# Transformer block on one core: first-group gate/up with plain products, second group nested as before, and another POOL cost in the planner

## The chip, the cores and the metric

The kernel runs on one core of a Trainium2 chip. The core has a matrix engine (TensorE, PE), a vector engine (VectorE, DVE), an activation engine (ScalarE, ACT), a general engine (GpSimd, POOL) and SyncE (SP), which issues most DMA transfers. Each engine has its own queue, and they wait for one another through semaphores. Matmul results land in PSUM, eight banks of 128 x 512 float32; all else on the core is in SBUF. The metric is the device time in microseconds (us) of one execution.

## What is computed

The reference is a block with modulation by a condition `c`, a linear attention and a gated feed-forward part, for 2048 rows of width 1024 and a hidden width of 3584:

```python
mod = (_silu(c) @ w_mod).reshape(c.shape[0], 6, 1, -1)   # sa, ca, ga, sb, cb, gb
h = _layernorm(x) * (1 + ca) + sa
x = x + ga * _A_ref(h, A_wqkv, A_wo)                     # linear attention, 32 heads
h = _layernorm(x) * (1 + cb) + sb
x = x + gb * _B_ref(h, B_w_gate, B_w_up, B_w_down)       # gelu(h @ w_gate) * (h @ w_up) @ w_down
```

The change lies in `h @ w_gate` and `h @ w_up`.

## The kernel before

**Order of the work.** All operations are first recorded in a plan (`Plan`). The matmuls of PE keep the order in which they were recorded. The orders of DVE, ACT, POOL and SP are worked out by the plan: `Plan.cost` gives each operation a cost, `sweep` runs a list schedule forward and backward over all operations, and the best order found is issued. So a cost that is changed for one engine can change the order on the other three, anywhere in the program. Helpers carry the line numbers: every DVE addition recorded through `tt_op` shows as L534, every copy of PSUM to SBUF through `fcopy` as L781.

**Stages.** First come queries, keys and values with the attention (`kvq_phase`, `merge_phase`), then the output projection with the second layer norm of the first group (`wo_phase`). Then, for each of two groups of 1024 rows, `gate_up(g)` and `down_out(g)`. The first group's gate/up has the late norm of the second group beside it (`late_norm`, one tile of 128 rows in a unit: ACT L1135, POOL L1136, ACT L1137, POOL L1138 to L1140, ACT L1141), and the preparation of weights for the down projection (`wd_sums`, in every other unit: ten DVE sums, whose results POOL stores to the scratch tensors `us` and `ts`; the SBUF slot for `us` is a single one).

**Products by Strassen and Winograd.** A product of two matrices, each in 2 x 2 blocks, is made with seven block products instead of eight, and sums of blocks before and after. `gate_up` runs over 14 units, gate and up in turn. A unit covers 256 hidden columns in two blocks, and each block product is eight matmuls: two halves e of 128 hidden columns (the weights are the stationary operand), four blocks of the contraction, and 512 rows moving (`mm_k`, L1284). The seven products of a unit are called P1 to P7 here; P1 is made at the end of the unit before it, beside P6 and P7. X, Z and Y are pairs of PSUM banks. P1 starts in Z, is copied from PSUM to PSUM by `seed` (ACT, L1338), and later products are added on both copies: P2 on one, P3, P4 and P6 one after another on the other, each read by ACT or DVE between (`direct`, `fcopy`, `comb`).

**Nested products.** A block product can itself be made with seven smaller ones (`Inner`, L1295): seven times two matmuls of 256 columns in the place of eight with 512. `INNER` says which products of a group are nested: before the change the first product, `b11`, in both groups (from unit 1 on) and the fifth, `t1`, in the second. A nested first product needs four more sums of weights per unit on DVE (`w_unit`), four sums of rows once per group (`rows_inner`), one PSUM copy (L1301) and two copies to SBUF on ACT, and two additions in PSUM on DVE (in `s32` and `s4`). Its steps are put between P6, P7 and the next unit's P2, and so are the two seeds: the last step `s6` and the second seed stand between P2(0) and P3(0) of the next unit.

Where the first product is plain, the branch that runs is:

```python
for e in range(2):
    mm_k(Z[e], w_next["a11"], e, h["b11"], True)
    P6(e)
    seed(X[e], Z[e])
P7(0)
P7(1)
```

**Memory.** SBUF is one tile, `mem`, that is cut by hand at offsets in KB. The sums of a nested product's rows lie at `yi_at`, those of its weights at `wi_rings` (from 7 and from 177). The `b11` quarter of the down projection's weights is loaded at 7 (`W_AT`), over the first of these rings.

Of the kernel before, what the change touches and what calls it, by code (L numbers as in the profile page):

```python
# [12 lines left out]
F16 = mybir.dt.float16  # L13
# [10 lines left out]
class Plan:  # L24
# [98 lines left out]
    def cost(self, op, outs, ins):  # L123

        size = lambda a: math.prod(d[1] for d in a.ap[1:])
        n = max(size(a) for a in (outs if op.eng == "PE" else outs + ins))
        psum = any(a.tensor.name.startswith("psum") for a in outs + ins)
        wide = any(a.dtype == FP32 and size(a) > 8 for a in outs + ins)
        ptrs = sum(size(a) == 1 for a in ins)
        if op.eng == "PE":  # L130
            op.cost = n / 2.4 + 2.5
            op.lat = op.cost + 165
            if op.fn == "matmul" and outs[0].ap[0][1] <= 32:
                op.cost /= 3.5
        elif op.fn.startswith("dma"):
            a = outs[0]
            op.cost, op.bytes = 1000 if op.eng == "POOL" else 450, math.prod(d[1] for d in a.ap) * (4 if a.dtype == FP32 else 2)
            op.bytes *= 2 if "accum_op" in op.kw else 1
            op.load = a.tensor.name.startswith("mem")
            if op.fn == "dma_start_transpose":  # L140
                op.cost, op.bytes = self.transpose
            op.lat = op.cost
        elif op.eng == "ACT":
            op.cost = (55 if psum else 112) + n / 1.2 + 85 * ptrs
            op.lat = op.cost + 115
            f = op.kw.get("func")
            op.table = "g" if f == AF.Gelu_apprx_tanh else "e" if f in (AF.Exp, AF.Ln) else None
        elif op.eng == "POOL":
            op.cost = op.lat = 700 + n / 0.5
        else:  # L150
            rate = 1.0
            if op.fn in ("tensor_scalar", "tensor_scalar_mul", "tensor_scalar_add", "tensor_copy") and not wide:
                rate = 1.0 if psum else 4.0
            elif op.fn == "tensor_tensor" and not wide:
                rate = 2.0
            op.cost = 69 + n / (0.96 * rate) + 61 * ptrs
            op.lat = op.cost + 83
# [119 lines left out]
def kernel(  # L277
# [39 lines left out]
    KH = KD // 2  # L317
# [57 lines left out]
    def at(off, shape, dt):  # L375
        return Ring(off, shape, dt, 1)()
# [43 lines left out]
    HB = TG // 2  # L420
# [42 lines left out]
    def quarters(n, shape, dt):  # L463
# [6 lines left out]
    f32_ring = Ring(158, [TG], FP32, 6)  # L470
    u_ring = Ring(170, [HB], FP32, 4)
    wi_rings = [Ring(7, [3, KH // 2, P], F16, 2), Ring(177, [3, KH // 2, P], F16, 2)]
    yi_at = [{"b11": at(174, [4, KH // 2, HB], F16)},
             {"b11": at(144, [4, KH // 2, HB], F16), "t1": at(148, [3, KH // 2, HB], F16)}]
    INNER = (("b11",), ("b11", "t1"))
    inner_done, h_inner = set(), {}
    p1v, p5v = at(158, [TT, NW], FP32), at(166, [TT, NW], FP32)
    c0_ring = Ring(174, [TG], F16, 3)
# [761 lines left out]
    def w_unit(g, n):  # L1240
# [12 lines left out]
        w = dict(a11=a11, a12=a12, a22=a22, s1=s1, s2=s2, s3=s3, s4=s4, inner={})  # L1253
        for name in INNER[g]:
            if n == 0 and name == "b11":
# [11 lines left out]
    def rows_inner(g):  # L1267
# [3 lines left out]
        inner_done.add(g)  # L1271
        for name in INNER[g]:
            y = h2[name]
# [445 lines left out]
```

## Time and profile before

| | |
|---|---|
| Median of 8 runs | 760.74 us (759.52 to 762.29) |
| Profiled execution, its own time | 760.0 us |
| Its span, first to last instruction | 758.2 us |
| PE busy | 735.7 us (97%), 4164 matmuls |
| DVE busy | 622.1 us (82%) |
| ACT busy | 412.4 us (54%) |
| POOL busy | 105.5 us (14%) |
| 128x512 matmul of L1284 | 1248, mean 379 ns |
| 128x256 matmul of L1295 | 560, mean 272 ns |
| Granted clock of TensorE | 1.00 |

[...]matmuls follow each other faster than they last, so the pace has to be read from their starts. The windows of a profile give the busy time of each engine in a stretch, in the order PE, weight loads (PEld), DVE, ACT, POOL, with the number of instructions, then clock, DMA share and GB/s. A line of the waits reads: who waited, for whom, total us, times, longest. In a timeline a bracket gives the idle time before an instruction and what ended it.

### The profile page before, as it was taken

How to read it: one execution, taken by the hardware profiler on the slowest of the kernel's cores; microseconds unless marked ns; L12 is line 12 of the kernel's file. 1: busy time of each engine (PE TensorE's matmuls, PEld its weight loads, DVE VectorE, ACT ScalarE, POOL GpSimd, SP SyncE). 2: the span in 40 equal slices, each digit the busy share in tenths (PEclk: the TensorE clock that was granted, in tenths of full speed). 3: DMA queues.
4: the chain of work that ended last, by engine and by line, in shares of the span. 5: the costliest groups of instructions: out<-in, count | busy, mean ns of one | idle time of the engine just before them, and what ended most of it. 6: DMA issues, size and time to landing. Idle time of an engine off the chain costs nothing.

```text
span 758.2 us, 11401 instructions
## 1 busy us (share of the span) xinstructions
PE 735.7 (97%) x4164; PEld 391.5 (52%) x4164; DVE 622.1 (82%) x1288; ACT 412.4 (54%) x697; POOL 105.5 (14%) x199
## 2 busy tenths in 40 slices
PE   5999999999999999989999999999999999999997
PEld 2454544453444445444445486645555555548664
DVE  7898986589897899899887779578889899897763
ACT  3675576668766578767565235016666666621000
POOL 1321433007121123141000001010000000000000
PEclk9999999999999999999999999999999999999999
DMA  9847167779389677876431999752323313399822
GB/s 314 299 116 248 38 154 165 291 293 173 98 235 324 210 261 277 295 256 216 131 107 49 288 288 301 257 185 87 112 64 104 112 57 112 101 271 293 272 110 75
DMA packets 140759, 144.78 MB, mean 191 GB/s; under 512 B 33440, under 2 KB 120864, under 8 KB 139936
## 3 DMA queue, kind: packets, MB, share of 16 engines
q1 hardware_dynamic: 124016, 106.31, 46.4%
q0 software_dynamic: 14336, 35.66, 14.8%
q10 hardware_dynamic: 2352, 2.10, 0.8%
q8 instruction: 32, 0.52, 0.3%
q14 instruction: 23, 0.19, 0.1%
HBM read 111.81 MB, written 32.24 MB: 190 GB/s over the span
## 4 chain that ended last, share of the span: by engine, by line
PE 76%; DVE 7%; ACT 5%; DMA 5%; issue 5%; POOL 1%; SPq 1%; POOLq 0%; DVEq 0%; ACTq 0%
PE psum L1284 25%; PE psum L1487 13%; PE psum L1531 8%; PE psum L836 6%; PE psum L1295 6%; PE psum L1176 6%; DVE mem L534 6%; PE psum L906 4%; PE psum L935 4%; DMA us<-mem 2%; DMA mem<-in_A_wqkv_dram 2%; DMA mem<-in_w_mod_dram 1%; PE psum L950 1%; PE psum L962 1%; DVE mem L975 1%
## 5 line engine op out<-in xcount | busy, mean ns | idle before, releaser
L534 DVE TENSOR_TENSOR mem<-mem 128x512 f16<-128x512 f16 (+11 forms) x633 | 291.9, 505 | 15.5 <-DMA us<-mem 5.4
L1284 PE MATMUL psum<-mem 128*128 128x512 f16 x1248 | 299.3, 379 | 2.8 <-ACT mem L781 1.0
L534 DVE TENSOR_TENSOR mem<-psum,mem 128x512 f16<-128x512 f32 (+4 forms) x260 | 192.1, 747 | 70.6 <-ACT mem L781 25.6
L781 ACT ACTIVATE mem<-psum 128x256 f32<-128x256 f32 (+2 forms) x228 | 123.3, 555 | 119.7 <-PE psum L1531 43.6
L1284 PEld LDWEIGHTS <-mem 128*128 128x128 f16 (+1 forms) x1248 | 122.0, 98 | 114.5 <-issue 5.2
L1487 PE MATMUL psum<-mem 128*128 128x512 f16 (+2 forms) x462 | 99.2, 373 | 0.5 <-DVE mem L534 0.5
L1295 PE MATMUL psum<-mem 128*128 128x256 f16 x560 | 89.5, 272 | 2.4 <-DVE psum L534 2.2
L1295 PEld LDWEIGHTS <-mem 128*128 128x128 f16 (+1 forms) x560 | 54.7, 98 | 48.1 <-issue 6.5
L1487 PEld LDWEIGHTS <-mem 128*128 128x128 f16 x462 | 45.2, 98 | 49.9 <-issue 0.7
L1338 ACT ACTIVATE psum<-psum 128x512 f32<-128x512 f32 x56 | 32.9, 587 | 62.1 <-PE psum L1284 31.5
L1531 PE MATMUL psum<-mem 128*128 128x256 f16 (+1 forms) x588 | 66.2, 273 | 0.0
L836 PE MATMUL psum<-mem 128*128 128x512 f16 (+1 forms) x280 | 62.5, 379 | 0.0
L1531 PEld LDWEIGHTS <-mem 128*128 128x128 f16 x588 | 57.6, 98 | 9.2
L1176 PE MATMUL psum<-mem 128*128 128x512 f16 x256 | 57.4, 379 | 0.6 <-DVE mem L534 0.6
L906 PE MATMUL psum<-mem 128*128 128x512 f16 x224 | 51.1, 379 | 0.1
L534 DVE TENSOR_TENSOR psum<-psum,mem 128x256 f32<-128x256 f32 x80 | 34.1, 426 | 11.6 <-ACT mem L781 11.5
L836 PEld LDWEIGHTS <-mem 128*128 128x128 f16 x280 | 27.0, 98 | 31.2
L1355 ACT ACTIVATE mem<-psum 128x512 f16<-128x512 f32 x56 | 33.3, 597 | 17.4 <-PE psum L1284 17.0
L1176 PEld LDWEIGHTS <-mem 128*128 128x128 bf16 x256 | 25.0, 98 | 31.0 <-issue 0.9
L906 PEld LDWEIGHTS <-mem 128*128 128x128 f16 (+1 forms) x224 | 21.5, 98 | 26.8 <-issue 2.1
L1365 ACT ACTIVATE mem<-mem 128x512 f16<-128x512 f16 x56 | 34.9, 629 | 0.5 <-DVE mem L534 0.3
L612 DVE BATCH_NORM_STATS2 mem<-mem 128x6 f32<-128x512 bf16 x48 | 30.9, 676 | 2.1 <-DMA mem<-in_A_x_dram 2.0
(127 smaller groups left out, 565.2 us busy)
## 6 DMA issues: line engine op xcount, KB each, us to landing
mem<-in_B_w_gate_dram SPq DMA_DIRECT2D x14, 1024.0 KB, 5.4
mem<-in_B_w_up_dram SPq DMA_DIRECT2D x14, 1024.0 KB, 5.9
mem<-in_w_mod_dram SPq DMA_DIRECT2D x24, 512.0 KB, 6.9
mem<-us SPq DMA_DIRECT2D x24, 448.0 KB, 8.0
mem<-in_A_x_dram SPq DMA_DIRECT2D x32, 256.0 KB, 3.7
ts<-in_B_w_down_dram POOLq DMA_DIRECT2D x28, 256.0 KB, 6.4
us<-mem POOLq DMA_DIRECT2D x7, 768.0 KB, 7.5
mem<-in_B_w_down_dram SPq DMA_DIRECT2D x12, 448.0 KB, 7.1
```

The lines of the kernel that those rows point to most:

```text
L534: ve.tensor_tensor(out=out, in0=a, in1=b, op=op)
L781: ac.activation(out=t, in_=ps, func=AF.Copy)
L836: te.matmul(ps, lhsT=A[:, k, i * P:(i + 1) * P], rhs=B[:, k, :], start=(start and k == 0), stop=(k == KH - 1), skip_group_check=True)
L906: te.matmul(o, lhsT=W[:, k, (j0 + i) * P:(j0 + i + 1) * P], rhs=h_form(a, k), start=(start and k == 0), stop=(k == KH - 1), skip_group_che ...
L1176: te.matmul(psw[:, half, :], lhsT=pqT[b][:, g, tl * P:(tl + 1) * P], rhs=Wp[:, g, half * NW:(half + 1) * NW], start=(g == 0), stop=(g == K ...
L1284: te.matmul(ps, lhsT=a[:, k, e, :], rhs=b[:, k, :], start=(start and k == 0), stop=(k == KH - 1), skip_group_check=True)
L1295: te.matmul(ps, lhsT=self.x[a][:, k, :], rhs=self.y[y][:, k, :], start=(start and k == 0), stop=(k == KH // 2 - 1), skip_group_check=True)
L1338: ac.activation(out=z, in_=x, func=AF.Copy)
L1355: ac.activation(out=o, in_=ps, func=AF.Gelu_apprx_tanh)
L1365: ac.activation(out=o, in_=o, func=AF.Gelu_apprx_tanh)
L1487: te.matmul(psm[:, q, c], lhsT=A[:, i, q * P:(q + 1) * P], rhs=wt[:, i, c], start=(start and i == 0), stop=(i == NPR - 1), skip_group_chec ...
L1531: te.matmul(ps[:, q, :], lhsT=a[:, k, q * P:(q + 1) * P], rhs=y[:, k, :], start=(start and q == 0 and k == 0), stop=(k == NPR // 2 - 1), s ...
```

## The change

The first group's gate/up makes all of its seven products with `mm_k`; the second group keeps the first and fifth nested. In the planner, a POOL operation of up to eight elements a partition is taken at 500 instead of about 702 ns, and larger ones at 250 + n / 0.46 instead of 700 + n / 0.5. Lines after 472 move up by one.

```diff
         elif op.eng == "POOL":
-            op.cost = op.lat = 700 + n / 0.5
+            op.cost = op.lat = 500 if n <= 8 else 250 + n / 0.46
...
     wi_rings = [Ring(7, [3, KH // 2, P], F16, 2), Ring(177, [3, KH // 2, P], F16, 2)]
-    yi_at = [{"b11": at(174, [4, KH // 2, HB], F16)},
-             {"b11": at(144, [4, KH // 2, HB], F16), "t1": at(148, [3, KH // 2, HB], F16)}]
-    INNER = (("b11",), ("b11", "t1"))
+    yi_at = [{}, {"b11": at(144, [4, KH // 2, HB], F16), "t1": at(148, [3, KH // 2, HB], F16)}]
+    INNER = ((), ("b11", "t1"))
```

In instructions: PE has 104 matmuls of 512 columns more and 182 of 256 fewer, DVE 82 instructions fewer, ACT 39 fewer; POOL and SP have as many as before.

## The prediction

> **What bounds the kernel now.** I first read the busy table and the chain of waits on the page: the chain that ended last is 76% TensorE (PE), and its largest line is L1284, the plain gate/up matmul. Then I took the busy time by stage. The stages were found by the first and last start of the lines that only one of them has. The last row is the second group, the first is the first group's gate/up, and the middle one is its down projection.
>
> ```profile
> core 0: us, PE busy (x) PEld busy (x) DVE busy (x) ACT busy (x) POOL busy (x), PEclk, DMA share, GB/s
> ...
> 253.50:427.50 174.00, 169.11 (x864) 84.33 (x863) 148.46 (x326) 117.63 (x220) 30.49 (x63) 1.00 0.62 206
> 427.50:508.00 80.50, 80.50 (x520) 50.66 (x518) 63.75 (x115) 19.62 (x30) 6.02 (x9) 1.00 0.86 254
> 508.00:673.40 165.40, 165.09 (x947) 92.44 (x946) 146.18 (x337) 106.13 (x221) 1.43 (x2) 1.00 0.36 108
> ```
>
> The reader should see that PE is at full clock and nearly always busy, but that the first group needs 174.0 us where the second, with more nesting, needs 165.4. To know how much of that is PE's own work I need the pace of one matmul, which the chain in order of time gives where PE runs freely:
>
> ```profile
> 340.54 1.73 PE psum L1284 x8
> ...
> 460.97 1.53 PE psum L1531 x14
> ```
>
> Eight matmuls with 512 columns take 1.73 us, 216 ns each; fourteen with 256 columns take 1.53 us, 109 ns each. In the first group unit 0 is plain, 56 x 216 = 12.1 us, and 13 units have six plain products and one nested: 48 x 216 + 14 x 109 = 11.9 us. That sums to 166.8 us, so 174.0 - 166.8 = 7.2 us are stalls. In the second group the same sum is 164.0 us, so only 1.4 us are stalls there, although two products are nested and DVE is 88% busy (146.2 of 165.4; first group 148.5 of 174.0, 85%).
>
> Where the 7.2 us are, I read from the starts of successive PE matmuls in the first group. Fifteen start more than 60 ns late, together 7.2 us. Laid against the kernel's PE order they are: six times the product P2(1) behind the seed copy on ACT, 0.26 to 0.42 us each, 1.9 us in all; six times the nested steps s7 and s6 behind the PSUM additions of s32 and s4 on DVE, 3.0 us in all; twice P7 behind DVE work of the unit, 1.2 us; once P6(0) behind a copy on ACT, 1.2 us. The table of waits shows the parts of these that stand out as idle PE, and what held DVE:
>
> ```profile
> PE psum L1295 <- DVE psum L534: 2.0, 4, 0.7
> PE psum L1284 <- ACT mem L781: 1.0, 1, 1.0
> PE psum L1284 <- DVE mem L534: 0.8, 2, 0.6
> PE psum L1284 <- ACT psum L1338: 0.7, 3, 0.3
> ...
> DVE mem L534 <- DMA us<-mem: 5.4, 3, 3.0
> ```
>
> One example of each, from the timeline:
>
> ```profile
> 269.47 0.61 ACT L1338 ACTIVATE psum<-psum 128x512 f32<-128x512 f32 x1
> 270.13 1.24 PE L1284 MATMUL psum<-mem 128*128 128x512 f16 x5 [0.25 <-ACT psum L1338]
> ...
> 327.75 0.42 DVE L534 TENSOR_TENSOR psum<-psum,mem 128x256 f32<-128x256 f32 x1
> 328.22 0.38 PE L1295 MATMUL psum<-mem 128*128 128x256 f16 x2 [0.51 <-DVE psum L534]
> ...
> 335.64 1.64 POOL L1136 TENSOR_SCALAR mem<-mem 128x1 f32<-128x1 f32 x1
> 337.31 1.15 ACT L1137 ACTIVATE mem<-mem 128x1024 f16<-128x1024 bf16 x1 [1.33 <-POOL mem L1136]
> 339.08 1.02 PE L1284 MATMUL psum<-mem 128*128 128x512 f16 x4 [1.00 <-ACT mem L781]
> ```
>
> The first two pairs are handovers that only the nested product has; the last triple is the late norm, POOL holding ACT and ACT holding a copy that PE needs.
>
> **What the Trainium skill says.** "TensorE: Matmul & The Clock Gate", section "Back-to-back issue gap", gives N/2.4 + 2.5 ns between matmuls, 109 ns for 256 columns and 216 ns for 512, and adds that a real stream at 512 runs at about 131 ns. The trace agrees with the formula and not with the 131. "Perfetto Trace Analysis", "Identifying the Most-Contended Engine", warns that matmul busy time is a bad measure; agreed here, as 169.1 us busy stand over 166.8 us of work and hide part of 7.2 us of stalls. "PSUM — Partial Sum Buffer", "Engine vs sequencer instructions", says that ScalarE, VectorE and GpSimdE queues are strictly first in, first out. The trace agrees: DVE stood 3.0 us at one addition for a `us` store and all behind it waited.
>
> **The change, part by part.**
>
> PE work. Removed: 13 units x 14 matmuls of 256 columns = 182 x 109 ns = 19.9 us. Added: 13 x 8 of 512 columns = 104 x 216 ns = 22.5 us. Net +2.6 us, all on the path, since PE sets the pace of this stage. The second group's PE order stays as it is.
>
> DVE. Removed per unit: four sums of weights, 128x256, 0.28 us each by the rows of that shape, and two PSUM additions of 0.43 us: 1.98 us, 25.7 us over 13 units; and the four sums of `rows_inner(0)`, 4 x 0.42 = 1.7 us. The stage's DVE time falls from 148.5 to about 123 us.
>
> ACT. Removed per unit two copies of 0.38 us and one PSUM copy of 0.37 us: 14.7 us in all. The two seed copies per unit, 0.59 us each, stay. Neither is PE time; their worth is in the stalls.
>
> Stalls that go. In the nested form the seed copy stands between s6 and P2(1) with one group of four matmuls (0.86 us) to cover it, and s32's and s4's addition, which follows a copy on ACT, has 1.73 us before s7 or s6. In the plain form seed(X[e]) follows P6(e), and five groups, 4.3 us, lie before the next unit's P2(e) needs it. ACT's or DVE's `direct` (0.60 or 0.69 us) comes first, then the seed (0.59 us): covered with 3 us to spare. If that cover goes, a late seed again costs its 0.3 to 0.4 us. So 1.9 + 3.0 = 4.9 us go. What is late next is the copy of P3 or P4, with 1.73 us before P4 or the following product overwrites its bank and 0.60 us to do; it is the plain part's tightest handover in both kernels.
>
> Stalls that stay. P7's 1.2 us and P6's 1.2 us come from DVE held by the single `us` buffer and from POOL and ACT in the late norm. Neither is removed. Bounds: 0 if the freed 2 us of DVE per unit let DVE catch up, 4.6 if they double. I take 2.3, unchanged.
>
> `rows_inner(0)`. Its four sums stand in DVE's queue during the output projection, right before the stretch in which the chain runs over DVE from 234.87 to 239.2 and PE then starts 0.81 us late at 239.27 behind a PSUM eviction. Taking 1.7 us out ahead of it should clear that: -0.8 us (bounds 0 and -0.8).
>
> POOL's cost in the planner, 702 to 500 ns for the one-column operations. It changes no instruction, only the orders of DVE, ACT, POOL and SP, and PE's not at all. The measured ones average 0.38 us (from 0.20 to 0.64 by row), so the planner still errs on the late side and ACT shouldn't stand at POOL more often. Orders before the first group move by a place or two; the number of matmuls between each release and its reader there is nearly the same in both. I take 0, bounds -1 and +2, two ACT operations of 1.06 us placed ahead of a needed copy.
>
> Loads. All of them remain, with the same sizes. `b11` of the down projection no longer waits for the nested weights' slot; before it was issued at 415.89, took about 7.2 us and was wanted at 427.5, so it is hidden in both.
>
> Sum: +2.6 - 4.9 - 0.8 = -3.1 us. The profiled execution, 758.2 us of span and 1.8 around it, 760.0 in all, becomes 756.9. The median shown, 760.74, lies 0.74 above, so I forecast 757.6 us.
>
> **The rivals.** About 0.2%, 1.5 us, is what a measurement of this kernel can tell from no change.
>
> A, forecast: nested-only stalls go, others stay: 757.6 us. Chance 0.55.
>
> B, the stalls go almost whole and the earlier stages gain: +2.6 - 7.2 - 0.8 = -5.4, 755.3 us. For it: DVE falls to about 72% of the stage. Against: the `us` wait and POOL's 1.64 us are not load. Chance 0.1.
>
> C, no change: part of what goes comes back at P3's and P4's copies, so that only about 2.6 of 8.0 us are gained: 760.7 us. For it: second group, with tighter handovers and the same DVE share, stalls only 1.4 us, so nesting alone is not the cause; a hold of 3.0 us on DVE is longer than any handover. Chance 0.2.
>
> D, slower: the cause of all first-group stalls is the hold by `us` stores and late norm, and the plain form merely takes it at another wait. The 7.2 us stay, nothing is gained at 239, and PE pays its 2.6 us: 763.3 us. It decides from where less than 1.1 us of stalls goes; the reordering's +2 would help it. Against: the six seed stalls recur in quiet units, at 270 and 408 too, with DVE not held. Chance 0.15.
>
> That the nested products stay in the first group is excluded by the order of instructions: PE has 78 matmuls fewer.
>
> **How the numbers follow.** A and B lie mainly in faster; A's own spread of about 1.7 us leaves a little to no change, D a little too. Faster 0.63, within 0.2% 0.21, slower 0.16. A's own range is 755.5 to 759.8. The wide one reaches from B, 755.4, into C and most of D: 755.4 to 762.8.
>
> **What would show it.** Right: the first group's gate/up lasts about 171.7 us with 169.3 us of matmul work (784 x 216 ns); waits on the seed and of L1295 on DVE are gone in it; DVE's busy time there is near 123 us; the late start at 239 is gone; the second group stays at 165.4. Wrong: stalls of over 5 us in the first group, at the writes after P3's and P4's copies or with DVE idle for `us`; or a stage before it that is over 1 us longer, which would put the reordering in the place of my zero.

## The result, and the profile after

The changed kernel takes 762.19 us (median of 18 runs, 759.52 to 763.99), the kernel before, run beside it, 759.6 us. The ratio is 1.0032, with a 95% interval of 1.0024 to 1.0040: slower by about 2.6 us, where I had forecast faster. The profiled execution took 763.52 us, 1.3 above the median, its span 761.7, against 760.0 and 758.2 before: 3.5 us more.

First the windows by stage, the view that the prediction shows for the kernel before, for the changed kernel: output projection, first group's gate/up, its down projection, second group's gate/up.

```profile
190.90:251.60 60.70, 60.23 (x280) 27.27 (x279) 50.26 (x80) 39.35 (x56) 11.97 (x22) 1.00 0.81 247
251.60:427.00 175.40, 171.65 (x785) 76.98 (x784) 129.60 (x248) 107.85 (x181) 34.90 (x63) 0.99 0.63 207
427.00:509.20 82.20, 80.58 (x519) 50.67 (x518) 67.67 (x126) 19.38 (x30) 6.03 (x9) 1.00 0.79 233
509.20:676.80 167.60, 165.77 (x948) 92.50 (x947) 140.26 (x326) 106.58 (x221) 1.42 (x2) 1.00 0.34 105
```

The first group's gate/up, where all removed instructions but the four sums of `rows_inner(0)` lay, is 1.6 us longer (175.45 by the starts of the first matmuls, 173.85 before). The two stages after it, which hold the same instructions as before, are longer too, by 1.8 us (82.22 for 80.44) and 2.1 us (167.57 for 165.46). PE reaches the gate/up 2.0 us earlier, at 251.55 for 253.51. The sum is -2.0 + 1.6 + 1.8 + 2.1 = +3.5 us. So 3.9 of the 5.5 us lost lie in stages from which the diff removes nothing, and the gain lies ahead of the gate/up, from where it removes only those four sums of DVE.

**The first group.** Matmul work is 169.3 us, as forecast, and the nested form's own stalls are gone. But 6.1 us of stalls stand in it, where I had left 2.3. Three lines of the waits of this stage:

```profile
ACT mem L1140 <- POOL mem L1139: 4.8, 4, 3.0
...
PE psum L1283 <- ACT mem L780: 3.6, 4, 2.2
ACT mem L1136 <- POOL mem L1135: 3.3, 4, 1.4
```

Before, ACT had one wait for POOL there:

```profile
ACT mem L1137 <- POOL mem L1136: 1.3, 1, 1.3
```

The place of the longest of PE's waits, in the timeline of the changed kernel:

```profile
344.35 1.06 ACT L780 ACTIVATE mem<-psum 128x512 f32<-128x512 f32 x2
344.52 0.75 POOL L1137 TENSOR_SCALAR mem<-mem 128x1 f32<-128x1 f32 x1 [1.35 <-ACT mem L1136]
...
345.99 0.60 POOL L1037 DMA_DIRECT2D us<-mem  x1 [0.72 <-DVE mem L533]
346.62 1.44 POOL L1138 TENSOR_TENSOR mem<-mem 128x1 f32<-128x1 f32 x1
348.14 0.26 POOL L1139 TENSOR_TENSOR mem<-mem 128x1 f32<-128x1 f32 x1
348.43 1.24 ACT L1140 ACTIVATE mem<-mem 128x1024 f16<-128x1024 bf16 x1 [3.02 <-POOL mem L1139]
349.58 1.06 ACT L780 ACTIVATE mem<-psum 128x512 f32<-128x512 f32 x2
...
350.21 8.11 PE L1283 MATMUL psum<-mem 128*128 128x512 f16 x29 [2.16 <-ACT mem L780]
```

Read it from the bottom. P6(0) waits for a copy of PSUM (L780) on ACT. The copy stands in ACT's queue right behind the late norm's L1140, which waits 3.02 us for POOL; and POOL had a store of `us` between two operations of the norm, which waited for DVE. From start to start the matmul is 2.3 us late. Three shorter waits for P3's copies add 1.7 us, and one more at P6 0.5 us. After the long one PE runs at half pace for a while, which costs another 1.7 us (the last section).

**The down projection.** PE has one stall in it. Here is ACT's part of the timeline, first before, then changed; L1156 and L1155 are the same line, the modulation of the second group's rows, which reads what the DMA transpose of the scratch tensor `xhs` brings.

```profile
447.29 0.60 ACT L781 ACTIVATE mem<-psum 128x512 f32<-128x512 f32 x1 [2.46 <-PE psum L1531]
448.81 0.60 ACT L781 ACTIVATE mem<-psum 128x512 f32<-128x512 f32 x1 [0.93 <-PE psum L1531]
449.31 3.62 ACT L1156 ACTIVATE mem<-mem 128x512 f16<-128x512 f16 x5
455.38 0.60 ACT L781 ACTIVATE mem<-psum 128x512 f32<-128x512 f32 x1 [2.45 <-DVE mem L534]
```

```profile
453.51 3.63 ACT L1155 ACTIVATE mem<-mem 128x512 f16<-128x512 f16 x5 [4.46 <-DMA mem<-xhs]
...
457.05 0.57 ACT L780 ACTIVATE mem<-psum 128x512 f32<-128x512 f32 x1
...
457.68 1.69 PE L1530 MATMUL psum<-mem 128*128 128x256 f16 x14 [1.61 <-ACT mem L780]
```

Five modulations wait 4.46 us for the transpose. The copy behind them starts 30.05 us after the stage's first matmul, where before it started after 28.02, and PE waits for this copy.

**The second group.** DVE waits for loads of weights five times, which it never did there before, and PE then waits for DVE or for ACT behind it. From the waits of the second gate/up, for all engines and for PE:

```profile
DVE mem L533 <- DMA mem<-in_B_w_gate_dram: 5.0, 5, 2.2
```

```profile
PE psum L1294 <- ACT psum L1300: 1.0, 3, 0.4
PE psum L1294 <- DVE psum L533: 0.7, 3, 0.3
```

Before, the table of PE's waits in this stage had one line, L1295 behind DVE, 0.2 us.

### The profile page after: what moved, and what is told of

Same layout as the page of the kernel before. It is cut to its first block, busy times and chain, and to the rows that moved or that the text cites. A ratio compares the mean times of both kernels' runs of the same rounds, so it can differ in the third digit from the quotient of the medians.

```text
span 761.7 us, 11075 instructions
## 1 busy us (share of the span) xinstructions
PE 739.1 (97%) x4086; PEld 384.0 (50%) x4086; DVE 600.5 (79%) x1206; ACT 402.6 (53%) x658; POOL 108.0 (14%) x199
## 4 chain that ended last, share of the span: by engine, by line
PE 74%; DVE 9%; DMA 7%; ACT 6%; issue 2%; POOL 1%; SPq 0%; DVEq 0%; POOLq 0%; ACTq 0%
PE psum L1283 25%; PE psum L1486 13%; DVE mem L533 7%; PE psum L1530 6%; PE psum L1175 6%; PE psum L905 5%; PE psum L835 5%; PE psum L1294 4%; PE psum L934 4%; DMA mem<-in_B_w_gate_dram 3%; PE psum L660 2%; DMA mem<-xhs 2%; DMA us<-mem 1%; PE psum L949 1%; DMA mem<-in_B_w_up_dram 1%
## 5 line engine op out<-in xcount | busy, mean ns | idle before, releaser
L1283 PE MATMUL psum<-mem 128*128 128x512 f16 x1352 | 312.4, 380 | 3.7 <-ACT mem L780 3.6
L533 DVE TENSOR_TENSOR mem<-mem 128x512 f16<-128x512 f16 (+12 forms) x577 | 279.6, 526 | 20.8 <-DMA mem<-in_B_w_gate_dram 7.4
L1283 PEld LDWEIGHTS <-mem 128*128 128x128 f16 (+1 forms) x1352 | 132.6, 98 | 142.2 <-issue 7.5
L780 ACT ACTIVATE mem<-psum 128x512 f32<-128x512 f32 (+2 forms) x202 | 112.9, 576 | 113.9 <-PE psum L1530 43.0
L1337 ACT ACTIVATE psum<-psum 128x512 f32<-128x512 f32 x56 | 32.7, 583 | 64.4 <-PE psum L1283 31.2
L1294 PE MATMUL psum<-mem 128*128 128x256 f16 x378 | 59.0, 272 | 1.8 <-ACT psum L1300 1.0
L1175 PE MATMUL psum<-mem 128*128 128x512 f16 x256 | 57.4, 379 | 0.5 <-DVE mem L533 0.5
L1294 PEld LDWEIGHTS <-mem 128*128 128x128 f16 (+1 forms) x378 | 36.9, 98 | 31.3 <-issue 5.3
L905 PE MATMUL psum<-mem 128*128 128x512 f16 x224 | 51.1, 379 | 0.3 <-ACT mem L850 0.2
L905 PEld LDWEIGHTS <-mem 128*128 128x128 f16 (+1 forms) x224 | 21.5, 98 | 27.2 <-issue 2.6
L533 DVE TENSOR_TENSOR psum<-psum,mem 128x256 f32<-128x256 f32 x54 | 23.0, 427 | 10.3 <-ACT mem L780 10.2
```

The lines of the kernel that those rows point to most:

```text
L533: ve.tensor_tensor(out=out, in0=a, in1=b, op=op)
L780: ac.activation(out=t, in_=ps, func=AF.Copy)
L905: te.matmul(o, lhsT=W[:, k, (j0 + i) * P:(j0 + i + 1) * P], rhs=h_form(a, k), start=(start and k == 0), stop=(k == KH - 1), skip_group_che ...
L1175: te.matmul(psw[:, half, :], lhsT=pqT[b][:, g, tl * P:(tl + 1) * P], rhs=Wp[:, g, half * NW:(half + 1) * NW], start=(g == 0), stop=(g == K ...
L1283: te.matmul(ps, lhsT=a[:, k, e, :], rhs=b[:, k, :], start=(start and k == 0), stop=(k == KH - 1), skip_group_check=True)
L1294: te.matmul(ps, lhsT=self.x[a][:, k, :], rhs=self.y[y][:, k, :], start=(start and k == 0), stop=(k == KH // 2 - 1), skip_group_check=True)
```

## The experiments

Theory 1: the loss is one of order. The plan works out anew what DVE, ACT, POOL and SP do after one another, over the whole program, whenever operations or a cost change; in the new order operations that wait for slow things (POOL, a transpose, a weight load) stand ahead of ones that PE needs. Rivals: the plain products as such bring new stalls, or the loads that now run earlier collide.

The stages of all runs, in us, from the starts of the first gate/up or down matmul in one profiled execution each; "start" is PE's arrival at the first gate/up. The second down projection took 81.3 in every one. With an unchanged order a stage still differs between executions: start by 2.2, the first gate/up by 1.4 (by 2.1 in the changed kernel's order), the down projection by 0.9 (by 1.3 in the old order, through e9), the second gate/up by 0.5. The medians are of 14 to 22 executions, in e6, e11 and e12 of five.

| kernel | start | gate/up 1 | down 1 | gate/up 2 | median | ratio to before, 95% |
|---|---|---|---|---|---|---|
| before | 253.51 | 173.85 | 80.44 | 165.46 | | |
| changed | 251.55 | 175.45 | 82.22 | 167.57 | 762.19 | 1.0032 (1.0024 to 1.0040) |
| e1 plain products only | 253.68 | 172.12 | 81.74 | 167.95 | 760.55 | 1.0010 (0.9998 to 1.0021) |
| e2 POOL cost only | 253.51 | 172.47 | 81.69 | 165.38 | 760.84 | 1.0032 (1.0014 to 1.0049) |
| e3 changed, old order after group 1 | 253.10 | 176.65 | 80.44 | 165.49 | 760.79 | 1.0015 (1.0004 to 1.0026) |
| e4 changed, copies ahead | 253.71 | 172.17 | 81.31 | 167.24 | 760.61 | 1.0023 (1.0014 to 1.0031) |
| e5 both | 253.34 | 172.64 | 80.44 | 165.46 | 758.39 | 0.9979 (0.9972 to 0.9987) |
| e6 before, new order after group 1 | 254.84 | 173.17 | 90.42 | 166.89 | 772.25 | 1.0173 (1.0151 to 1.0195) |
| e7 as e3, ACT alone | 251.72 | 174.58 | 80.71 | 167.76 | 761.34 | 1.0028 (1.0019 to 1.0038) |
| e8 as e3, DVE alone | 251.86 | 174.55 | 81.56 | 165.46 | 760.46 | 1.0016 (1.0007 to 1.0025) |
| e9 plain products, old order | 253.82 | 173.13 | 81.73 | 165.48 | 759.24 | 0.9993 (0.9986 to 1.0001) |
| e10 before, new order ahead | 252.15 | 172.44 | 80.44 | 165.48 | 758.31 | 0.9980 (0.9972 to 0.9987) |
| e11 e9 with early seed | 253.56 | 169.86 | 80.44 | 165.48 | 756.01 | 0.9947 (0.9932 to 0.9961) |
| e12 e11 and e10's order | 252.70 | 169.75 | 80.69 | 165.48 | 755.43 | 0.9943 (0.9930 to 0.9956) |

**The two halves of the change, e1 and e2.** The changed kernel with the old POOL cost, and the kernel before with the new one:

```diff
-            op.cost = op.lat = 500 if n <= 8 else 250 + n / 0.46
+            op.cost = op.lat = 700 + n / 0.5
```

```diff
-            op.cost = op.lat = 700 + n / 0.5
+            op.cost = op.lat = 500 if n <= 8 else 250 + n / 0.46
```

> The first group's products plain, the planner's POOL cost as before. Theory 1 (the loss sits in the orders that the planner gives down projection and second group, and the plain products alone tip them): the orders after the first group are almost those of the changed kernel, so its 1.8 us in the first down projection and about 2 us in the second group return, and the ratio to before is 1.002 to 1.006. Theory 2 (the POOL cost tips them): those two stages are as before, 80.4 and 165.5 us, and the ratio is 0.997 to 1.000.

> The first group nested as before, only the planner's POOL cost as in the change. Theory 1: the orders after the first group become those of the changed kernel here too (ACT's differs from it in 4 of 276 places), so the first down projection takes about 82.2 us and the second group about 167.5, the stages before the first group may win up to 2 us, ratio 1.000 to 1.005. Theory 2': without plain products nothing but the early stages moves, ratio 0.997 to 0.999.

e1 as a whole is not to be told from the kernel before, below the 1.002 to 1.006 that the theory gave. By stages its profile, an execution 1.7 us above the median, fits: the first gate/up gains 1.7 us, near what I had forecast for it (2.3), and the two stages after it lose 1.3 and 2.5 us, at the same waits as in the changed kernel (ACT 4.0 us for the transpose with PE 1.1 us behind it; DVE 5.4 us for `w_gate`). So the plain products are enough to upset the order of later stages: the planner's new cost isn't needed for that.

The new cost alone (e2) upsets the down projection by 1.3 us (ACT 4.6 us for the transpose, PE 1.1 us behind it), not the second group, where the theory had expected 2 us. e2's ratio, 1.0032, isn't explained by its profile: that execution took 759.79 us, and three of the 18, of which no trace was kept, took 767.1 to 767.3; their cause stays open. Neither half by itself gives the 175.45 us of the first gate/up.

**The old order after the first group, e3.** Operations were given a written order, in the place of the planned one; everything that belongs to later stages is in the sequence of the kernel before on DVE, ACT, SP and POOL.

```diff
-            for op in self.order():
+            for op in written(self.ops, ORDER):
```

> The changed kernel with the orders of DVE, ACT, POOL and SP written out; all work recorded after the first group's gate/up stands in the order that the kernel before gives it. Theory 1: the first down projection is back at 80.4 us and the second group at about 165.5, so 3.5 to 4 us less than the changed kernel, ratio to before 0.996 to 0.999. Rival (the loads and transposes merely land late because the first group ends at another time, whatever the order): the stages keep 82.2 and 167.5 us, ratio 1.002 to 1.004.

The windows of the two later stages in e3:

```profile
429.75:510.19 80.44, 80.33 (x517) 50.71 (x518) 63.71 (x116) 19.62 (x30) 6.01 (x9) 1.00 0.83 247
510.19:675.68 165.49, 165.18 (x947) 92.53 (x946) 146.37 (x337) 106.08 (x221) 1.43 (x2) 1.00 0.35 108
```

Both are back at 80.44 and 165.49, with the plain products and their earlier loads still in place. That the order makes these 3.9 us is shown here. The whole gained less than the 3.5 to 4 us expected, 1.4 us by medians. In this execution PE came 1.6 us later to the first gate/up and spent 1.2 us more in it, both within what one order varies by; why the medians gain so little stays open.

**One engine at a time, e7 and e8.** As e3, but with ACT alone, or DVE alone, in the old order. ACT's queue in the down projection, changed kernel against e7 (L780 a PSUM copy, L1155 the modulation), is the core of it:

```diff
+L780 Activation mem<-psum 128x512 x4
+L1155 Activation mem<-mem 128x512 x5
 L780 Activation mem<-psum 128x512
 L1155 Activation mem<-mem 128x512 x3
 L780 Activation mem<-psum 128x512
-L1155 Activation mem<-mem 128x512 x4
-L780 Activation mem<-psum 128x512
 L1155 Activation mem<-mem 128x512
-L780 Activation mem<-psum 128x512
-L1155 Activation mem<-mem 128x512 x5
...
```

> The changed kernel with ACT alone in the old order after the first group's gate/up. Theory (the down projection's loss is ACT's order, the second group's is DVE's): down projection 80.4 us, second gate/up still 167.6: -1.8 us against the changed kernel. Rival (the transposes' place on SP sets both): the down projection stays at 82.2.

> The changed kernel with DVE alone in the old order after the first group's gate/up. Theory (as in the run with ACT alone): down projection still 82.2 us, second gate/up 165.5: -2.1 us against the changed kernel. Rival (the weight sums are late because the gate weights' loads stand later on SP, not because of DVE's order): second gate/up stays at 167.6.

By stages it is as the theory had it: ACT's order restores the down projection (80.71) and not the second group (167.76); DVE's restores the second group (165.46) and leaves the down projection at 81.56. The rivals, SP's order of transposes or of weight loads, fall: SP kept its new order in both. By medians the two are 0.9 and 1.7 us below the changed kernel, for 1.8 and 2.1 expected.

**The copies ahead of the late norm, e4.** In the first group, up to two PSUM copies that stood right behind an operation of the late norm on ACT were put ahead of it, 29 moves in all, such as:

```diff
-L1140 Activation mem<-mem 128x1024
 L780 Activation mem<-psum 128x512 x2
+L1140 Activation mem<-mem 128x1024
```

> The changed kernel with its orders written out; in the first group each ACT operation of the late norm that stands right before copies of PSUM is put behind up to two of these. Theory 1: the waits of PE for ACT copies in the first group (2.3, 0.7, 0.8, 0.5, 0.3 us) go, and with the longest idle stretch the slow matmuls after it (1.9 us), so the first group lasts 170 to 171.5 us and the time is 4 to 6 us below the changed kernel, ratio 0.995 to 0.998. Rival (the late norm is only pushed and the hold on DVE for us stores shows at other copies): the first group stays at 174 us or more, ratio 1.001 or more.

The first gate/up falls from 175.45 to 172.17 us. So its excess was that order as well, not the plain products. What stays are two waits of P7 behind DVE, 2.2 us, one of 1.9, where DVE itself is held by the late norm. The time as a whole missed the 4 to 6 us expected: by medians it is 1.6 us below the changed kernel. In this execution PE came 2.2 us later to the stage.

**Both, e5.**

> The changed kernel with both orders written out that were tried singly: after the first group's gate/up DVE, ACT, SP and POOL take the order of the kernel before, and inside it up to two PSUM copies stand ahead of each late-norm operation of ACT. Theory (the added loss is order, and its parts are separate): first group's gate/up 172.2 us, its down projection 80.4, second group's gate/up 165.5, so 763.5 - 3.3 - 1.8 - 2.1 = 756.3 in a profile like the changed kernel's, a median near 757 and a ratio of 0.995 to 0.998 to the kernel before: faster, as I had forecast. Rival (what is saved at one place is given back at the next because another limit stands behind both): a median of 760 or more, the ratio 1.000 or above, with one of the three stages 1.5 us or more above its value here.

758.39 us: the changed kernel with these orders put right is faster than the kernel before (0.9979), and the three stages are within 0.5 us of what was expected. The rival falls.

**The other way round, e6.** The kernel before with the changed kernel's order after the first group.

> The kernel before, with the order that the changed kernel has after the first group's gate/up on DVE, ACT, SP and POOL. Theory (order alone makes the loss): down projection of the first group 82.2 us in the place of 80.4, gate/up of the second group 167.6 in the place of 165.5, so +3.9 us, a ratio of about 1.005. Rival (the order only hurts where the first group before it is plain and DVE and ACT arrive early): both stages as before, ratio 1.000.

The order does harm there too, so the rival falls; but it costs 12.8 us, three times what I expected, 10 of them in the down projection. The trace says why. SP's queue issues the transposes behind the load of `b11` of the down projection's weights (L1483, L1482 in the changed kernel). From SP's timeline, e6 first, then the changed kernel:

```profile
416.54 0.37 SPq L1483 DMA_DIRECT2D mem<-in_B_w_down_dram  x1
...
439.20 6.04 SPq L1114 DMA_TRANSPOSE mem<-xhs  x1
...
449.79 10.81 SPq L1114 DMA_TRANSPOSE mem<-xhs  x1
```

```profile
403.02 0.37 SPq L1482 DMA_DIRECT2D mem<-in_B_w_down_dram  x1
...
426.66 6.64 SPq L1113 DMA_TRANSPOSE mem<-xhs  x1
...
440.71 7.55 SPq L1113 DMA_TRANSPOSE mem<-xhs  x1
```

With nested products `b11` waits for their slot in SBUF (it is issued at 415.89 us in the kernel before and at 416.54 in e6, with plain products at 403.02 in the new order and 404.65 in the old, e9), and all behind it in SP's queue waits too. The new order of ACT was made for transposes that come some 9 to 13 us earlier. In e6 ACT meets them late, and PE behind it:

```profile
448.82 2.22 ACT L1156 ACTIVATE mem<-mem 128x512 f16<-128x512 f16 x3 [6.40 <-DMA mem<-xhs]
450.94 0.57 ACT L781 ACTIVATE mem<-psum 128x512 f32<-128x512 f32 x1
```

```profile
451.57 13.67 PE L1531 MATMUL psum<-mem 128*128 128x256 f16 x98 [5.20 <-ACT mem L781]
```

**My sum alone, e9.** The plain products with the order of the kernel before everywhere; only the nested product's operations are taken out of the queues.

> The changed kernel's products in the order of the kernel before, throughout: DVE, ACT, SP and POOL keep the old sequence, from which only the operations of the nested product are taken out. So this is the sum of my forecast by itself, with its zero for the planner made true. Theory (the working was right but for that zero): first group's gate/up 171.7 us (169.3 of matmuls and 2.3 of stalls), its down projection 80.4, second gate/up 165.5, 756.9 in a profile like that of before, a ratio of 0.995 to 0.998: faster. Rival (the stalls of the nested form come back at other waits even in the old order, my rival C or D): gate/up of the first group 173.5 or more, ratio 0.999 or above.

The theory falls, and the rival is right in the ratio alone: 0.9993, no change to speak of. The first gate/up is at 173.13 us, between the two, 3.8 us of it stalls, and not at P3 or P4, as my rival C had it. PE's only waits in that stage, by the table:

```profile
PE psum L1283 <- ACT psum L1337: 2.1, 7, 0.3
```

L1337 is the seed. My forecast took the seed's stall for one that only the nested form has. In this kernel the form is plain and the seed keeps the late place in ACT's queue that the nested form gave it, and P2(1) waits for it in nine units (0.29 to 0.47 us from start to start; the table's idle times are shorter). The down projection had one wait of 1.1 us for `ts`, which the same order didn't have in e3, e5 and e11; its cause was not tried.

**The seed moved up, e11.** The second seed of each unit stands right behind the first, or behind P6(1)'s gelu copy where that comes between; 13 moves, of this kind:

```diff
-L1337 Activation psum<-psum 128x512
+L1337 Activation psum<-psum 128x512 x2
 L1364 Activation mem<-mem 128x512
 L1140 Activation mem<-mem 128x1024
 L1364 Activation mem<-mem 128x512
-L1337 Activation psum<-psum 128x512
 L780 Activation mem<-psum 128x512
...
```

> As the run with the plain products in the old order throughout, but the second seed of each unit of the first group, which had kept the late place on ACT that the nested form gives it, stands directly behind the first seed, or behind the gelu copy of P6(1) where that comes between. Theory (3.8 us of the 3.8 us of stalls left in the first group were the seed's place in ACT's queue): first gate/up 169.5 to 170.3 us in the place of 173.1, the rest as there, a ratio of 0.994 to 0.997: this is the gain that I had put down to the plain form. Rival (with the seed early ACT or DVE is late at another wait, the copies of P3 or P4): first gate/up 172 or more, ratio about 0.998 or above.

The windows of e11, first gate/up and after it, and PE's only wait from 250 to 520 us:

```profile
253.56:423.42 169.86, 169.38 (x785) 76.74 (x784) 130.31 (x249) 107.51 (x181) 30.47 (x63) 1.00 0.63 209
423.42:503.86 80.44, 80.44 (x519) 50.66 (x518) 63.71 (x116) 19.62 (x30) 6.02 (x9) 1.00 0.84 247
```

```profile
PE psum L1283 <- ACT mem L780: 0.5, 1, 0.5
```

The stage is at its matmul work but for this one wait (0.65 us from start to start): 169.86 us. The kernel takes 756.01 us, 3.9 less than the one before (0.9947). This is about the gain that I had put down to the plain form; it takes the seed's early place as well.

**The order ahead of the first group, e10 and e12.** The kernel before with the changed kernel's order up to the first gate/up, and e11 with the same.

> The kernel before, with the order that the changed kernel has ahead of the first group's gate/up on DVE, ACT, SP and POOL. Theory (the 2.0 us that the changed kernel's profile gained ahead of the gate/up are not the order's; five later profiles with that same order show 189.0 to 190.9 us there, the kernel before 190.5): ratio 0.999 to 1.001, first stage within 1 us of 190.5. Rival (the order gains them): first stage 188.6, ratio 0.9975.

> The same, and ahead of the first group's gate/up the order of the changed kernel, which by itself took the kernel before to 0.998. Theory (the parts add up): 1.3 us less than the run with the early seed alone, a ratio of 0.992 to 0.995, about 755 us: faster than both kernels. Rival (they don't add: an earlier start of the gate/up only moves the waits for the us stores and the transposes): the same ratio as the run with the early seed alone.

In e10 my theory falls and the rival is right: 758.31 us, 0.9980, 1.3 us gained. PE's waits ahead of 254 us, before:

```profile
PE psum L962 <- ACT mem L965: 1.9, 2, 1.0
PE psum L606 <- DMA mem<-in_w_mod_dram: 0.8, 1, 0.8
```

and in e10, which has no wait on `w_mod` left in the table:

```profile
PE psum L962 <- ACT mem L965: 1.1, 2, 0.9
```

I had been misled by PE's arrival in single executions, which differs by 2.2 us with one and the same order: 22 executions told it, one profile did not. Over the profiles with one of these two orders PE arrives at 252.5 us on average with the new one ahead (eight kernels) and at 253.9 with the old one (before, e6, e9, e11). e12 has the lowest median of all, 755.43 us, 0.9943, and so beats both kernels; but it isn't told apart from e11 (0.9947), so whether the 1.3 us add to the rest stays open.

## Why the prediction was wrong

By its own steps, against the profiled execution: I had -2.3 for the first gate/up, -0.8 ahead of it and 0 after it, -3.1 in all. Measured were +1.6, -2.0 and +3.9, and by medians the loss is 2.6 us.

**PE work, +2.6: right.** e11 without the late part of its one wait leaves 169.86 - 0.65 = 169.2 us of matmul work; forecast 169.3. (182 x 109 ns is 19.8 us, not 19.9; the net stays.)

**Stalls that go, -4.9: right for the changed kernel, and for 1.9 of it by a reason that isn't sufficient.** The waits at the nested steps s7 and s6 can't occur and don't. The seed's 1.9 us are gone in the changed kernel too, whose planned order has the second seed directly behind the first in six of 13 units; in e9 it never stands there. I had "covered with 3 us to spare" from the order in which the products are recorded; e9 shows 3.8 us of waits on the seed in the plain form, where ACT's order holds it late. That the 1.9 us went in the changed kernel was luck as far as my reason goes.

**"Stalls that stay ... I take 2.3, unchanged": the step that failed first.** They became 6.1 us, above the upper bound of 4.6 that I gave. I had taken the late norm's hold as a thing of POOL and DVE that this change doesn't touch. It is a thing of ACT's order: with it put right the stage takes 3.3 us less (e4), and with the old order and an early seed all stalls but one of 0.65 us go (e11). So the bound below, 0, was nearer to what the form allows than the value taken.

**"POOL's cost in the planner ... I take 0", and no term at all for the stages after the first group: the step that failed second, and the larger.** The bounds were -1 and +2. The reason given, that ACT "shouldn't stand at POOL more often", is wrong: in the first gate/up it stood there once for 1.3 us before and eight times for 8.1 us after, by the tables of waits. e1 without the new cost has 3.3 us of this and e2 with it alone 1.2, so in these profiles it took both halves of the change. I had compared orders only ahead of the first group, and asked only what the cost change would do; the second group's PE order does stay, but PE waits there for engines whose order doesn't. But 121 operations of DVE and ACT had gone from the list that the planner sorts, and e1 shows that this alone reorders the later stages, in its profile to a loss of 3.8 us. DVE's order after the first group differs in 404 of 558 places; I did not look at it. How many places differ isn't the measure, though: in e2 it is 414, and its second group takes 165.38 us. Ahead of the first group, where I looked, the "place or two" were worth -1.3 us (e10). Why the planner's search settles on the worse orders was not looked into.

**`rows_inner(0)`, -0.8: at most about a quarter of it came.** The late start near the end of that stage is 0.63 us in the changed kernel for 0.81; with the old order it is 0.76 (e9) and 0.60 (e11).

**DVE's busy time**, forecast near 123 us, was 129.6. I had subtracted 25.7 us of row durations from a window's busy time. In the traces the durations of successive DVE instructions overlap by some 0.08 us (starts 0.60 apart, 0.68 long), and the window counts covered time once: 148.5 - 129.6 = 18.9 us for 78 instructions.

**Rival D** gave 763.3 us, where the median is 762.19 and the profiled execution took 763.5. This is luck for the most part, since only part of its mechanism is there: a late-norm hold is taken at another wait, yet over half of the loss lies in stages that no rival of mine named.

## What to carry to other kernels

Where a scheduler lays out queues, a change that removes operations can change every queue to the end of the program, as it did here: compare the orders in all stages, and in each queue look for operations that wait on a slow producer (a transpose, a load, a chain over two engines) directly ahead of one that the bounding engine needs. Ask of a stall that "goes" which order makes it go: the seed's stall belonged to a place in ACT's queue, not to the nested form. And to learn what such a change is worth, hold the old order and take out only what it removes, then mend single places.

## What the runs showed of the hardware

After its longest waits in these stages PE fell to half pace. The windows of the changed kernel around the wait that ends at 350.21 us, where the sixth figure after the length is the granted clock:

```profile
350.20:351.40 1.20, 1.19 (x6) 0.56 (x6) 1.20 (x3) 0.45 (x1) 0.38 (x1) 0.93 0.28 99
351.40:354.60 3.20, 3.20 (x9) 1.10 (x8) 1.84 (x6) 0.58 (x1) 0.00 (x0) 0.50 0.14 50
354.60:360.00 5.40, 5.40 (x26) 2.45 (x25) 5.23 (x14) 1.92 (x4) 0.46 (x1) 1.00 0.62 196
```

PE first runs at its full pace for about 1.1 us, five matmuls. Then for 3.2 us the clock is 0.50, and seven matmuls of 512 columns start 427 ns apart instead of 216; together with the two at the edges 1.7 us are lost, after a wait of 2.16 us. The same came after waits of 2.49 us in e3, 2.16 in e7 and 2.01 in e8. In e6, after 5.20 us, matmuls of 256 columns started 213 ns apart for 27 in a row, where 109 is the pace, which lost 2.8 us. After 1.91 us of idle time, in e4 and in e5, the pace was 216 ns at once and stayed so.

The Trainium skill, "TensorE: Matmul & The Clock Gate", section "Part 1: The HAM clock gate (the "warmup" mystery)", has the half rate after an idle window of about 3.4 us; the trace agrees with the half rate, which lasted 3.3 us in one case and 5.8 (27 x 213 ns) in the other, but here 2.01 us of idle time (e8) were enough to bring it. In the changed kernel a wait of 2.16 us so cost nearly twice what it lasts: 2.3 us of lateness and 1.7 of half pace.

One-column operations of POOL have very different durations in the profile: in the changed kernel's first gate/up they take from 0.18 to 1.64 us. The three longest (1.44 for L1138 above; 1.63 and 1.64) stand right behind the issue of a store, but others that stand there take 0.18 and 0.34. What makes them long isn't shown.
